# First loads and steps of a three-layer mixer in another order, the softmax over positions split off, state rows last in the first quarter

## The chip, the cores and the metric

The kernel runs on one core of one Trainium2 chip. The metric is the device time of that core in microseconds (us). In this text PE is TensorE, DVE VectorE, ACT ScalarE, POOL GpSimd and SP the engine that issues the loads and stores.

## The reference, cut to what matters

```python
def reference(x, state, moe_w_in, moe_w_out, moe_alpha, moe2_w_in, moe2_w_out):
    # x [4, 8, 512, 64], state [4, 8, 32, 64]
    s = 0.125 * x @ state.T                       # [4, 8, 512, 32]
    xread = softmax_over_states(s) @ state        # [4, 8, 512, 64]
    sread = softmax_over_positions(s.T) @ x       # [4, 8, 32, 64]
    t = concat([xread, sread], axis=2)            # 544 rows of a batch
    t = t.transpose(0, 2, 1, 3).reshape(4 * 544, 512)
    h = t @ moe_w_in                              # 512 -> 2048
    t = (max(h, 0) + moe_alpha * min(h, 0)) @ moe_w_out    # -> 512
    h = t @ moe2_w_in
    return (max(h, 0) + log1p(exp(-abs(h)))) @ moe2_w_out
```

A softmax has 1e-9 added to its sum. The four weights are 64-bit floats in memory; x, the state and alpha are 32-bit floats.

## The kernel before, in words

**Three layers in one pass.** Attention between 512 positions and 32 state rows of each of 8 heads and 4 batches gives 4 x 544 token rows of 512 numbers. Two feed-forward layers follow (m = 0 with leaky relu, m = 1 with softplus), each 512 to 2048 to 512. Each of their inner dimensions is worked through in NQ = 4 quarters of 512; in a quarter `hidden` computes a tile of 128 inner columns (fc = 0 to 3) for one block of 512 tokens (b = 0 to 3, the positions of a batch), or, for the block B, all 512 inner columns for the 128 state rows; `act` applies the nonlinearity and `out_part` multiplies by the second weight and adds into the running output. `out_part` runs LAG = 3 tiles behind.

**Accuracy.** TensorE's products are made of three: `mm3` (L136 to L138) multiplies high by high, low by high and high by low, and `split` makes the two parts, the high one on ACT (L142) and the low one on DVE or POOL (L145).

**Weights.** They come in 64 tiles of 128 x 512, each a load of 512 KB of 8-byte words into one of three staging buffers (`wload`, L188). `wconv` turns one into 32-bit floats: two steps on ACT (L202 exp, L203 top), three on DVE (L204, L205, L206) and one on POOL (L207), through one buffer `exp` and one buffer `top`. It then issues the next `wload`, which waits for the staging buffer. `wprep` (letter p) converts if needed and splits; the four tiles of the first weight in layer 0 (wi0h, wi0l, wi1h, wi1l for the first quarter) stay whole. The output weights of the first quarter (wo0 to wo3) follow them.

**Attention.** A step i is a batch and a group of four heads: i = 2 * batch + group, eight steps. It uses one of three sets of scratch tiles, i % 3; for i % 3 = 0 these are acc tiles, for 1 the tiles wo4 to wo6, for 2 further acc tiles and wi4, at7l. The parts, with their letters in the tables, are:

- x: `at_load_t` (L250), two loads of 256 KB of the transposed x; y: `at_load_x` (L254), two loads of x.
- s: `at_scores` (L269 to L275): eight matmuls give scores in PSUM, ACT copies them (L270), DVE takes their maximum over the positions (L271) and makes the bias (L272), ACT takes the exponent with its sum (L273), DVE adds the 1e-9 and takes the reciprocal (L274, L275).
- r: `at_rows` (L283 to L292): four transposes of the copied scores, the softmax over the states on DVE, ACT (L288) and POOL (L292).
- b: `at_back` (L299): transposes back and splits into at0h, at0l and so on. d: `at_read` (L308 to L330): transposes the exponents, multiplies by x (L314), scales (L323), transposes (L324), copies into the state rows (L330, srh).
- w: `sw_batch` (L238), the state times the first weight (tiles sw0h, sw0l and so on): `hidden` multiplies the probabilities by that product, so a block needs its own and its batch's steps.

**What sets the order.** Tables in the code do: LOADS and BEFORE list parts ahead of the first hidden tile, AMONG those ahead of the n-th hidden tile of the first quarter; SPLIT and SPLIT_FIRST say after which tiles a weight is prepared, SW_AHEAD and SW_LAST where the state-weight batches of later quarters go. A scheduler arranges each engine's queue from them once, when the program is built; each engine then runs its queue in order and waits on semaphores. All loads and stores stand in SP's queue.

## Time and profile of the kernel before

| quantity | us |
|---|---|
| median of three timed runs | 753.73 (753.58 to 754.25) |
| profiled execution, its own time | 752.3 |
| span of the profiled execution | 750.5 |
| PE busy (share of the span) | 727.6 (97%) |
| DVE busy | 425.3 (57%) |
| ACT busy | 423.2 (56%) |
| POOL busy | 170.5 (23%) |

The profiled execution is one run recorded by the hardware. Its span goes from the first to the last recorded instruction; 1.8 us of its time lie outside. The shares are averages over the whole span, so the rows further down take it stretch by stretch, and then instruction by instruction where an engine stands idle.

### The profile page before, as it was taken

The numbers are of one execution on the slowest core, as the hardware profiler recorded it, in microseconds if no ns is written. First come the engines' busy times: TensorE is split into PE (matmuls) and PEld (weight loads), VectorE is DVE, ScalarE is ACT, GpSimd is POOL, SyncE is SP. The second block draws the span as 40 slices with busy tenths as digits, with TensorE's granted clock in tenths as the row PEclk, the third lists the DMA queues.
The fourth block names the chain that finished last, engine by engine and source line by source line (L and its number), as shares of the span: only waits on it lengthen the run. The fifth ranks groups of instructions, "written<-read, shape, count | busy, mean of one in ns | idle before, by whom it ended". The sixth has DMA issues, their size and how long they took to land.

```text
span 750.5 us, 9504 instructions
## 1 busy us (share of the span) xinstructions
PE 727.6 (97%) x3580; PEld 561.7 (75%) x3580; DVE 425.3 (57%) x693; ACT 423.2 (56%) x764; POOL 170.5 (23%) x142
## 2 busy tenths in 40 slices
PE   5699998999999999999999999999999999999998
PEld 2267665777777777878888888888888888888886
DVE  4898657757778447885575224654257342333433
ACT  4778767735554335554677647755466354444560
POOL 2352332402142003452571003410044000000000
PEclk9989999999999999999999999999999999999999
DMA  9654313203211001220122001220010000001102
GB/s 323 221 174 156 107 44 115 85 7 108 83 57 57 0 1 58 86 82 1 56 79 91 0 1 57 84 85 1 0 57 0 1 1 0 1 1 56 57 15 112
DMA packets 16654, 47.27 MB, mean 63 GB/s; under 512 B 2016, under 2 KB 2016, under 8 KB 16608
## 3 DMA queue, kind: packets, MB, share of 16 engines
q1 hardware_dynamic: 16608, 46.66, 18.4%
q8 instruction: 28, 0.46, 0.3%
q14 instruction: 18, 0.15, 0.1%
HBM read 42.20 MB, written 4.46 MB: 62 GB/s over the span
## 4 chain that ended last, share of the span: by engine, by line
PE 94%; DVE 2%; ACT 2%; DMA 1%; issue 1%; POOL 0%; SPq 0%; ACTq 0%
PE pb L136 17%; PE pb L138 17%; PE pb L137 17%; PE pa L136 13%; PE pa L137 12%; PE pa L138 12%; PE pa L238 2%; PE pa L359 2%; PE pa L269 1%; DMA acc<-xt 1%; DVE top L204 1%; PE pa L367 0%; ACT exp L202 0%; PE pb L269 0%; ACT top L203 0%
## 5 line engine op out<-in xcount | busy, mean ns | idle before, releaser
L386 DVE SCALAR_TENSOR_TENSOR pa<-pa,tmp 128x512 f32<-128x512 f32 x68 | 47.4, 697 | 128.8 <-ACT tmp L385 128.8
L383 ACT ACTIVATE tmp<-pa 128x512 f32<-128x512 f32 x68 | 40.5, 596 | 92.7 <-PE pa L138 73.0
L429 DVE TENSOR_TENSOR acc<-pb,acc 128x512 f32<-128x512 f32 x102 | 67.4, 686 | 37.4 <-PE pb L138 37.4
L204 DVE SCALAR_TENSOR_TENSOR top<-stg,top 128x512 uint16<-128x512 uint16 x64 | 53.0, 828 | 46.8 <-ACT top L203 46.2
L207 POOL TENSOR_TENSOR cnv<-top,cnv 128x512 f32<-128x512 bf16 x48 | 56.4, 1175 | 101.0 <-DVE cnv L206 97.2
L379 DVE SCALAR_TENSOR_TENSOR pa<-tmp,rest,pa 128x512 f32<-128x512 f32 (+1 forms) x80 | 53.2, 671 | 25.7 <-ACT tmp L375 25.2
L202 ACT ACTIVATE exp<-stg 128x512 bf16<-128x512 bf16 x64 | 42.9, 671 | 38.7 <-DVE cnv L206 28.6
L375 ACT ACTIVATE tmp<-pa 128x512 f32<-128x512 f32 x68 | 40.2, 596 | 43.0 <-PE pa L138 36.4
L203 ACT ACTIVATE top<-exp,top_bias 128x512 uint16<-128x512 uint16 x64 | 46.1, 721 | 9.2 <-POOL cnv L207 5.5
L385 ACT ACTIVATE tmp<-tmp 128x512 f32<-128x512 f32 x68 | 42.9, 630 | 1.7
L384 ACT ACTIVATE tmp<-tmp 128x512 f32<-128x512 f32 x68 | 42.9, 631 | 1.5
L206 DVE SCALAR_TENSOR_TENSOR cnv<-stg,exp 128x512 f32<-128x512 uint32 x48 | 35.8, 745 | 13.0 <-POOL wo5l L145 4.1
L205 DVE TENSOR_SCALAR exp<-top 128x512 uint16<-128x512 uint16 x64 | 32.1, 502 | 1.1
L142 ACT ACTIVATE g1h<-pa 128x512 fp32r<-128x512 f32 x33 | 19.7, 596 | 20.8 <-DVE pa L386 12.4
L142 ACT ACTIVATE g3h<-pa 128x512 fp32r<-128x512 f32 x33 | 19.7, 596 | 19.3 <-DVE pa L379 9.6
L142 ACT ACTIVATE g0h<-pa 128x512 fp32r<-128x512 f32 x33 | 19.6, 594 | 19.1 <-DVE pa L379 10.2
L145 DVE TENSOR_TENSOR g3l<-pa,g3h 128x512 fp32r<-128x512 f32 x33 | 22.7, 689 | 13.4 <-ACT g3h L142 13.2
L145 DVE TENSOR_TENSOR g1l<-pa,g1h 128x512 fp32r<-128x512 f32 x33 | 22.7, 688 | 12.7 <-ACT g1h L142 12.3
L145 DVE TENSOR_TENSOR g0l<-pa,g0h 128x512 fp32r<-128x512 f32 x33 | 22.7, 688 | 10.5 <-ACT g0h L142 10.1
L145 DVE TENSOR_TENSOR g2l<-pa,g2h 128x512 fp32r<-128x512 f32 x33 | 22.7, 687 | 10.0 <-ACT g2h L142 9.9
L142 ACT ACTIVATE g2h<-pa 128x512 fp32r<-128x512 f32 x33 | 19.7, 597 | 14.5 <-DVE pa L386 7.6
L145 POOL TENSOR_TENSOR wo3l<-cnv,wo3h 128x512 fp32r<-128x512 f32 x5 | 6.5, 1294 | 76.1 <-ACT wo3h L142 75.9
(863 smaller groups left out, 2119.7 us busy)
## 6 DMA issues: line engine op xcount, KB each, us to landing
stg<-w1i SPq DMA_DIRECT2D x16, 511.8 KB, 4.0
stg<-w1o SPq DMA_DIRECT2D x16, 511.8 KB, 3.4
stg<-w2i SPq DMA_DIRECT2D x16, 511.8 KB, 3.9
stg<-w2o SPq DMA_DIRECT2D x16, 511.8 KB, 3.3
out<-acc SPq DMA_DIRECT2D x16, 256.0 KB, 2.0
acc<-xt SPq DMA_DIRECT2D x10, 256.0 KB, 4.8
acc<-xs SPq DMA_DIRECT2D x8, 256.0 KB, 5.3
wo4h<-xt SPq DMA_DIRECT2D x3, 256.0 KB, 3.5
```

Of the source, the lines that this page charges most:

```text
L136: nc.tensor.matmul(ps, lh, rh, start=start, stop=False)
L137: nc.tensor.matmul(ps, lh, rl, start=False, stop=False)
L138: nc.tensor.matmul(ps, ll, rh, start=False, stop=stop)
L142: nc.scalar.activation(h, src, AF.Copy)
L145: eng_l.tensor_tensor(out=l, in0=src, in1=h, op=ALU.subtract)
L202: nc.scalar.activation(e, top.bitcast(BF16), AF.Abs)
L203: nc.scalar.activation(tu, eu, AF.Relu, bias=top_bias, scale=TOP_SCALE)
L204: nc.vector.scalar_tensor_tensor(out=tu, in0=top, scalar=TOP_SIGN, in1=tu, op0=ALU.bitwise_and, op1=ALU.bitwise_or)
L207: nc.gpsimd.tensor_tensor(out=a, in0=t, in1=a, op=ALU.add)
L379: nc.vector.scalar_tensor_tensor(out=ps[:, cs], in0=t[:, cs], scalar=a, in1=ps[:, cs], op0=ALU.mult, op1=ALU.add)
L386: nc.vector.scalar_tensor_tensor(out=ps, in0=ps, scalar=0.0, in1=t, op0=ALU.max, op1=ALU.add)
L429: nc.vector.tensor_tensor(out=a, in0=ps, in1=a, op=ALU.add)
```

## The change

LOADS now brings the transposed x of steps 0 and 1 around the first weight tiles and x of step 0, and no more. BEFORE has 12 entries where it had 27: weights, scores, rows and transposes back of steps 0 and 1, the first state-weight batch and the load of step 2. The rest is spread over 13 entries of AMONG. A new part, letter e, `at_positions`, holds the softmax over the positions, which was the end of `at_scores`; it reads the copy of the scores, not PSUM. Its two small operations that make the bias and add the 1e-9, and the one of `at_rows` that adds the 1e-9, go from DVE to POOL. The block of the state rows is the last one in the first quarter instead of the fourth. In the first quarter conversions stop at 16 tiles. The state-weight batches of blocks 2 and 3 come after the hidden tiles 5 and 9, and the second quarter has a table of its own for preparing weights.

```diff
--- before.py
+++ after.py
@@ -43,11 +43,16 @@
 
 
 
-LOADS = "L0 x0 L0 y0 x1 L0 x2 y2 y1"
-BEFORE = "p0 s0 c0 s1 r0 p0 c0 r1 d0 b0 p0 x3 d1 y3 p0 w0 b1 p0 y4 s2 p0 r2 c0 x4 s3 w1 c0"
-AMONG = ("d2 r3 b2", "d3 s4 x5", "b3", "r4", "s5 y5 p0 d4 x6", "p0 r5 s6", "y6 d5 r6 b4 b5", "", "y7 x7 s7 d6", "b6 r7", "d7 b7")
-
-SPLIT_FIRST = (9, 10, 11, 12, 13, 14, 15, 16)
+LOADS = "L0 x0 L0 x1 L0 y0"
+BEFORE = "p0 s0 p0 s1 r0 p0 r1 x2 b0 p0 w0 b1"
+AMONG = (
+    "y1 e0 d0 s2 r2 p0", "x3 s3 e1 d1 p0 b2", "y3 y2 r3 p0", "b3 w1 p0",
+    "e2 d2 x4 y4", "e3 d3 x5 y5 s4 r4", "s5 r5 b4", "b5 e4 d4 x6 y6",
+    "e5 d5 x7 y7 s6 r6", "s7 r7 b6", "b7", "e6 d6", "e7 d7",
+)
+
+SPLIT_FIRST = (9, 10, 11, 12, 13, 14, 15)
+SPLIT_SECOND = (2, 3, 4, 5, 7, 9, 10, 12, 16)
 SPLIT = (1, 2, 4, 5, 7, 9, 10, 16)
 
 SW_AHEAD = (10, 13, 15)
@@ -261,17 +266,21 @@
     def at_scores(i):
 
         b, g = i // 2, i % 2
-        t, n2 = scratch(i), st_n[i % 3]
+        t = scratch(i)
         ps = bank(pool_s(i))
         for k in range(2):
             for hh in range(2):
                 r, o = slice(hh * D, (hh + 1) * D), col(g, k, hh)
                 nc.tensor.matmul(ps[o : o + NS], stf.f[r, head(2 * g + k, b)], t[k][r], start=True, stop=True)
         nc.scalar.activation(t[4], ps, AF.Copy)
-        nc.vector.tensor_reduce(out=n2[:, 0:1], in_=ps, op=ALU.max, axis=AX.X)
-        nc.vector.tensor_scalar(n2[:, 0:1], n2[:, 0:1], -SCALE, None, op0=ALU.mult)
-        nc.scalar.activation(t[5], ps, AF.Exp, bias=n2[:, 0:1], scale=SCALE, accum_out=n2[:, 1:2])
-        nc.vector.tensor_scalar(n2[:, 1:2], n2[:, 1:2], EPS, None, op0=ALU.add)
+
+    def at_positions(i):
+
+        t, n2 = scratch(i), st_n[i % 3]
+        nc.vector.tensor_reduce(out=n2[:, 0:1], in_=t[4], op=ALU.max, axis=AX.X)
+        nc.gpsimd.tensor_scalar(n2[:, 0:1], n2[:, 0:1], -SCALE, None, op0=ALU.mult)
+        nc.scalar.activation(t[5], t[4], AF.Exp, bias=n2[:, 0:1], scale=SCALE, accum_out=n2[:, 1:2])
+        nc.gpsimd.tensor_scalar(n2[:, 1:2], n2[:, 1:2], EPS, None, op0=ALU.add)
         nc.vector.reciprocal(n2[:, 1:2], n2[:, 1:2])
 
     def at_rows(i):
@@ -287,7 +296,7 @@
         nc.vector.tensor_tensor(out=e3, in0=p3, in1=m1.to_broadcast([P, 16, NS]), op=ALU.subtract)
         nc.scalar.activation(e1, e1, AF.Exp, scale=SCALE)
         nc.vector.tensor_reduce(out=s1, in_=e3, op=ALU.add, axis=AX.X)
-        nc.vector.tensor_scalar(s1, s1, EPS, None, op0=ALU.add)
+        nc.gpsimd.tensor_scalar(s1, s1, EPS, None, op0=ALU.add)
         nc.vector.reciprocal(s1, s1)
         nc.gpsimd.tensor_tensor(out=e3, in0=e3, in1=s1.to_broadcast([P, 16, NS]), op=ALU.mult)
 
@@ -454,6 +463,8 @@
             i = int(x[1:])
             if x[0] == "s":
                 at_scores(i)
+            elif x[0] == "e":
+                at_positions(i)
             elif x[0] == "r":
                 at_rows(i)
             elif x[0] == "d":
@@ -488,7 +499,7 @@
     for m in range(2):
         for q in range(NQ):
             first = m == 0 and q == 0
-            blocks = (0, 1, 2, B, 3) if first else (0, 1, B, 2, 3)
+            blocks = (0, 1, 2, 3, B) if first else (0, 1, B, 2, 3)
             n = 0
             for b in blocks:
                 for fc in range(4 if b < B else 1):
@@ -502,15 +513,16 @@
                     if len(todo) >= LAG:
                         out_part(*todo.pop(0))
                     todo.append((m, q, b, fc, g))
-                    wconv()
+                    if not first or nconv[0] < 4 * NQ:
+                        wconv()
                     if m == 0:
                         if n in SW_AHEAD and q < NQ - 1:
                             sw_batch(q + 1, SW_AHEAD.index(n))
-                        if first and b in (0, 1) and fc == 2:
-                            sw_batch(q, b + 2)
+                        if first and n in (5, 9):
+                            sw_batch(q, 2 + (n == 9))
                         if not first and n == SW_LAST:
                             sw_batch(q, B - 1)
-                    if n in (SPLIT_FIRST if first else SPLIT):
+                    if n in (SPLIT_FIRST if first else SPLIT_SECOND if (m, q) == (0, 1) else SPLIT):
                         wprep()
                     n += 1
     for job in todo:
```

The tables alone do not say where an instruction stands, since the scheduler arranges it. Three places of the built program follow, first before and then after. Operand names carry buffer numbers (pa and pb are PSUM banks); lines of after are 5 to 9 higher than the same lines of before (L136 is L141, L238 is L243, L283 is L292, L308 is L317).

PE around the first hidden tile (the matmuls with at0h, sw0h to at1h, sw1l; acc_99, acc_100 and at7l are steps 2 and 3's tiles, wi0h to wi1l the first weights, ex0h the state), before:

```order
L324 MATMUL pb_247<-ident,wo4h 128x128
L238 MATMUL pa_281<-wi1l,ex0h 32x512 x2
L269 MATMUL pb_363<-acc_95,ex0h 32x512 x2
L269 MATMUL pb_363<-acc_96,ex0h 32x512 x2
L283 MATMUL pa_342<-ident,wi4l 128x128 x4
L238 MATMUL pa_374<-wi0h,ex0h 32x512 x2
L238 MATMUL pa_374<-wi0l,ex0h 32x512 x2
L238 MATMUL pa_375<-wi1h,ex0h 32x512 x2
L238 MATMUL pa_375<-wi1l,ex0h 32x512 x2
L308 MATMUL pa_399<-ident,at7l 128x128 x4
L283 MATMUL pa_428<-ident,acc_99 128x128 x4
L136 MATMUL pa_449<-at0h,sw0h 128x512
```

and after:

```order
L243 MATMUL pa_204<-wi1l,ex0h 32x512 x2
L141 MATMUL pa_296<-at0h,sw0h 128x512
L142 MATMUL pa_296<-at0l,sw0h 128x512
L143 MATMUL pa_296<-at0h,sw0l 128x512
L333 MATMUL pa_243<-ident,acc_95 128x128
L141 MATMUL pa_296<-at1h,sw1h 128x512
L142 MATMUL pa_296<-at1l,sw1h 128x512
L143 MATMUL pa_296<-at1h,sw1l 128x512
L317 MATMUL pa_329<-ident,wo6l 128x128 x4
L274 MATMUL pb_318<-acc_95,ex0h 32x512 x2
L274 MATMUL pb_318<-acc_96,ex0h 32x512 x2
L323 MATMUL pb_335<-wo5h,wo6h 32x64 x8
```

Before, the scores of step 3 (acc_95, acc_96), the batch of block 1 (the two pairs L238) and the transposes of step 2's exponents (at7l) stand ahead of the first hidden tile; after, the first hidden tile comes right behind wi1l, and step 3's scores (L274) right behind it.

SP's queue, where step 3's loads are acc_95 and acc_96 from xt, and stg_64 to stg_66 are the staging buffers, before:

```order
L254 DMA acc_97<-xs 128x512
L254 DMA acc_98<-xs 128x512
L250 DMA acc_96<-xt 128x512
L188 DMA stg_66<-w1o 128x2047
L250 DMA acc_95<-xt 128x512
L254 DMA wo5h<-xs 128x512
L254 DMA wo5l<-xs 128x512
L188 DMA stg_64<-w1o 128x2047
L250 DMA wo4l<-xt 128x512
L188 DMA stg_65<-w1o 128x2047
```

and after:

```order
L193 DMA stg_65<-w1o 128x2047
L255 DMA acc_96<-xt 128x512
L193 DMA stg_66<-w1o 128x2047
L193 DMA stg_64<-w1o 128x2047
L255 DMA wo4l<-xt 128x512
L259 DMA acc_97<-xs 128x512
L259 DMA acc_98<-xs 128x512
L193 DMA stg_65<-w1o 128x2047
L255 DMA acc_95<-xt 128x512
L259 DMA wo5h<-xs 128x512
L259 DMA wo5l<-xs 128x512
```

Before, acc_95's load comes ahead of the loads into wo5h, wo5l and stg_64; after, it stands behind the second load into stg_65 of this list.

ACT's queue where the second gate tile's high half (g1h) is made, before:

```order
L202 ACTIVATE exp_75<-stg_65 128x512
L270 ACTIVATE wo6h<-pa_499 128x512
L142 ACTIVATE g0h<-pa_449 128x512
L203 ACTIVATE top_74<-exp_75,top_bias 128x512
L142 ACTIVATE wo2h<-cnv_69 128x512
L375 ACTIVATE tmp_72<-pa_512 128x512
L142 ACTIVATE at2h<-pb_440 128x512
L330 ACTIVATE srh<-pb_405 64x32 x4
L273 ACTIVATE wo6l,stn_84<-pa_499,stn_84 128x512
L323 ACTIVATE acc_95<-pb_476,stn_83 128x128
L375 ACTIVATE tmp_73<-pa_542 128x512
L142 ACTIVATE g1h<-pa_512 128x512
```

and after:

```order
L339 ACTIVATE srh<-pb_335 64x32 x4
L147 ACTIVATE at2h<-pa_362 128x512
L147 ACTIVATE wo1h<-cnv_68 128x512
L208 ACTIVATE top_74<-exp_75,top_bias 128x512
L282 ACTIVATE acc_100,stn_83<-acc_99,stn_83 128x512
L297 ACTIVATE acc_96<-acc_96 128x512
L384 ACTIVATE tmp_72<-pa_371 128x512
L384 ACTIVATE tmp_73<-pa_411 128x512
L207 ACTIVATE exp_75<-stg_65 128x512
L147 ACTIVATE wo2h<-cnv_69 128x512
L208 ACTIVATE top_74<-exp_75,top_bias 128x512
L147 ACTIVATE g1h<-pa_371 128x512
```

After, the second and third hidden tiles (tmp_72, tmp_73) are passed on next to each other, and a conversion's exp, a split and top stand between them and g1h; before, read-out parts and scores stood there.

## Rows read from the trace of the kernel before

**Rows 1.** Stretches: length, busy us of PE, PEld, DVE, ACT, POOL; clock, DMA.

```profile
0.00:38.15 38.15, 22.62 (x173) 9.49 (x174) 25.44 (x59) 24.21 (x51) 11.45 (x16) 0.95 0.77 269
38.15:92.90 54.75, 54.66 (x426) 36.60 (x424) 45.86 (x90) 42.13 (x96) 20.72 (x18) 0.97 0.44 145
92.90:121.50 28.60, 25.05 (x159) 16.92 (x158) 17.94 (x34) 19.78 (x44) 8.71 (x8) 1.00 0.22 74
121.50:345.00 223.50, 223.50 (x1064) 169.93 (x1065) 154.66 (x246) 117.17 (x202) 63.97 (x50) 1.00 0.18 57
```

**Rows 2.** Waits of PE, 0 to 130 us: total, times, longest.

```profile
PE pa L136 <- DVE g1l L145: 2.4, 1, 2.4
...
PE pa L136 <- ACT srh L330: 1.2, 1, 1.2
```

**Rows 3.** Timeline of PE: start, us, line, operands, count, idle before.

```profile
25.96 0.62 PE L238 MATMUL pa<-wi1l,ex0h 64*32 64x512 f32 x2 [1.38 <-POOL wi1l L207]
...
26.43 1.44 PE L269 MATMUL pb<-acc,ex0h 64*32 64x512 f32 x6
...
27.80 0.66 PE L283 MATMUL pa<-ident,wi4l 128*128 128x128 f32 x4
...
28.38 0.62 PE L238 MATMUL pa<-wi0h,ex0h 64*32 64x512 f32 x2
...
29.57 0.60 PE L238 MATMUL pa<-wi1l,ex0h 64*32 64x512 f32 x2
...
37.72 0.63 PE L138 MATMUL pa<-at1h,sw1l 128*128 128x512 f32 x1
...
104.45 0.62 PE L238 MATMUL pa<-wi2h,ex0h 64*32 64x512 f32 x2
...
105.47 0.50 PE L136 MATMUL pa<-at4h,sw4h 128*128 128x512 f32 x1
```

**Rows 4.** Stretch of 2 us around the first hidden tile; clock after POOL's busy time.

```profile
36.00:38.00 2.00, 2.00 (x6) 1.55 (x5) 2.00 (x8) 2.00 (x5) 0.31 (x2) 0.50 0.68 240
```

**Rows 5.** Page, groups: busy us, mean ns; conversion (L202 to L207), splits.

```profile
L204 DVE SCALAR_TENSOR_TENSOR top<-stg,top 128x512 uint16<-128x512 uint16 x64 | 53.0, 828 | 46.8 <-ACT top L203 46.2
...
L207 POOL TENSOR_TENSOR cnv<-top,cnv 128x512 f32<-128x512 bf16 x48 | 56.4, 1175 | 101.0 <-DVE cnv L206 97.2
...
L202 ACT ACTIVATE exp<-stg 128x512 bf16<-128x512 bf16 x64 | 42.9, 671 | 38.7 <-DVE cnv L206 28.6
...
L203 ACT ACTIVATE top<-exp,top_bias 128x512 uint16<-128x512 uint16 x64 | 46.1, 721 | 9.2 <-POOL cnv L207 5.5
...
L206 DVE SCALAR_TENSOR_TENSOR cnv<-stg,exp 128x512 f32<-128x512 uint32 x48 | 35.8, 745 | 13.0 <-POOL wo5l L145 4.1
...
L205 DVE TENSOR_SCALAR exp<-top 128x512 uint16<-128x512 uint16 x64 | 32.1, 502 | 1.1
...
L142 ACT ACTIVATE g1h<-pa 128x512 fp32r<-128x512 f32 x33 | 19.7, 596 | 20.8 <-DVE pa L386 12.4
...
L145 DVE TENSOR_TENSOR g1l<-pa,g1h 128x512 fp32r<-128x512 f32 x33 | 22.7, 688 | 12.7 <-ACT g1h L142 12.3
```

**Rows 6.** Timeline of DVE: third step of two successive conversions.

```profile
34.10 0.67 DVE L206 SCALAR_TENSOR_TENSOR cnv<-stg,exp 128x512 f32<-128x512 uint32 x1
...
41.10 0.68 DVE L206 SCALAR_TENSOR_TENSOR cnv<-stg,exp 128x512 f32<-128x512 uint32 x1
```

**Rows 7.** Timeline of the load queue (SP): first half of step 3.

```profile
20.29 0.38 SPq L250 DMA_DIRECT2D acc<-xt  x1
```

**Rows 8.** Page, DMA issues: KB each, us from issue to landing.

```profile
acc<-xt SPq DMA_DIRECT2D x10, 256.0 KB, 4.8
...
wo4h<-xt SPq DMA_DIRECT2D x3, 256.0 KB, 3.5
```

**Rows 9.** Groups by form, DVE and POOL: busy us, mean ns.

```profile
L272 DVE TENSOR_SCALAR stn<-stn 128x1 f32<-128x1 f32 x8 | 1.2, 148 | 0.1
...
L547 POOL MEMSET const-float32-1.0<- 128x1 f32 x1 | 0.1, 98 | 0.0
```

## The prediction

> **What bounds the kernel now.** I read the busy time of the engines by stretches first [rows 1]. From 121.5 to 345 us TensorE (PE) is busy for all 223.5 of 223.5 us. Nothing that this change does to an order can shorten that: from about 150 us to the end PE's queue is the same, instruction for instruction. What can be won or lost lies ahead of that. From 0 to 38.15 us, where the first hidden tile is finished, PE is busy for 22.62 us, so 15.5 are idle; from 38.15 to 92.9 it idles 0.09; and from 92.9 to 121.5 it idles 28.60 - 25.05 = 3.55. The waits of PE by releaser [rows 2] name these last 3.55 us: 1.2 for the copies of the state read-out on ACT (srh), 2.4 for the low half of a gate tile on DVE (g1l). Both stand around the state rows' block. So the question is how early PE can begin a row of matmuls without a hole. In that sense the start bounds the kernel, and behind it stand ACT and DVE, which prepare everything that PE reads: in 38.15 to 92.9 they are busy 42.13 and 45.86 of 54.75 us, 77% and 84% [rows 1]. They have room, but not much.
>
> **The change, part by part.** The sum is made against the profiled execution, 752.3 us, of which 1.8 lie outside the span of 750.5; the median of the three timed runs is 1.43 above it (753.73).
>
> *An earlier first hidden tile.* Its last operand in the new order is the low half of the second state-weight tile, and that hangs on the fourth weight tile, wi1l. In the kernel before PE gets that tile at 25.96 [rows 3]; less work stands ahead of it now (the read-out of step 1 and the scores of steps 2 and 3 are partly behind it), and walking the queues I find it at about 25.55, an estimate. Then come, in the order of ACT's and DVE's queues, the next weight tile's conversion up to its third DVE step and only then the split: 0.72 + 0.83 + 0.50 + 0.75 + 0.69 [rows 5], and one matmul of 0.43, from 37.72 to the end of the hidden tile at 38.15 [rows 3]. Sum 3.9, so 29.5 instead of 38.15. With four transposes that follow (some 0.5) PE stands at 30.0. But work that was done before 38.15 is now still open: the scores of step 3 (27.80 - 26.43, about 1.4), the transposes of its rows and those of step 2's exponents (0.58 each, 28.38 - 27.80), the read-out of step 1 (about 0.8, estimated from instruction counts), and the state-weight batch of block 1, between 1.0 (105.47 - 104.45, when all four weights are ready and four matmuls stand abreast) and 1.8 (28.38 to 30.17, two abreast) [rows 3]. I take 1.0, together 4.4. **Lead: 38.15 - 30.0 - 4.4 = 3.75 us.** Its bounds: 2.5 with the dearer batch and wi1l as late as before, 4.8 if wi1l comes 1 us earlier still.
>
> *The state rows' block at the end of the first quarter.* Its read-out now has block 3's matmuls as cover, and the 1.2 and 2.4 us of [rows 2] go: **3.55 us gained**. What covers them: the out-matmuls of block 3, twelve of the 512-column kind for each gate tile; if they run out, up to 2.4 come back.
>
> *A new wait for step 3's inputs.* This is what the move costs on the queue of loads. In the kernel before the first half of step 3's load is issued at 20.29 [rows 7]. Now it stands behind the load of a weight tile that has to wait for a staging buffer, which DVE's third step of the first output-weight tile sets free. That step I put at 28.7 (wi1l's successor, by the conversion's own steps), so the load goes out at about 29.15, since one issue takes 0.4. It lands 3.5 us later as the lone 256 KB load does, or 4.8 as such loads do in the middle [rows 8]: 32.7 to 34.0. PE's scores of step 3 stand directly behind the first hidden tile, and ahead of the second and third, so PE is held from 30.0 to **32.7: 2.7 us lost**, at most 4.0. I take the lower end because only the weight load of the moment is beside it. Behind the waiting scores stand the whole of block 0's remaining hidden tiles, which need nothing of step 3.
>
> *Waits for gate tiles and read-outs that stand behind conversions.* The weight conversion goes round through single buffers: 0.72 and 0.83 + 0.50 + 0.75 + 1.18 make 3.97 us [rows 5], with the handovers and one or two splits of 0.60 between them 5.1 to 5.6, an estimate; in the kernel before two successive third steps lie 41.10 - 34.10 = 7.0 apart [rows 6]. PE is now some 4 us ahead but the conversions aren't, and gate tiles stand behind them in ACT's queue: the second gate tile behind exp, a split and top (0.67 + 0.60 + 0.72 [rows 5]), then its own 0.60 [rows 5], 2.6 and with handovers 2.7 to 3.2 after DVE's third step. Third steps at 40.1, 50.8 and 60.0 give 43.25 for the second gate tile, 53.5 for the fourth and 63.25 for a read-out's copies. PE would be ready at 41.5, 52.1 and 61.7: **1.7, 1.4 and 1.55 us lost**. Later, where the softmax and read-outs of batches 2 and 3 come closer together, I take **1.0** more, near the 1.2 that such a copy cost before [rows 2]; between 0 and 1.6. For all four together (5.65) the bounds are 0, if the conversions keep step, and about 7.
>
> *State-weight batches of the second quarter.* They fall on a moment at which their four weights come one after the other, so pairs instead of fours: 1.79 instead of 1.02 [rows 3], **0.7 lost**; between 0 and 0.8.
>
> *The split softmax, and small operations on GpSimd.* The exponent of the positions is a function of its own now, but on ACT it stands at rows 7, 12 and 20 for the first three steps (6, 13 and 32 before): it is hardly put off. I cost it at nothing; what hides it is that PE has transposes and scores of other steps beside it, and uncovered it is 0.7. Twenty-four small operations go from DVE to GpSimd: 0.148 us each on DVE [rows 9], 8 of them a little more. That frees some 4 us of DVE over 100 us, none of it on the path by itself. What one costs on GpSimd the trace doesn't show; the nearest row is a fill of the same shape, 0.10 us [rows 9], and the far end is a tile-wide operation there, 1.18 [rows 5]. I take the near one, for the shape: nothing on the path, at the far end 1 us once, on step 0.
>
> The Trainium skill, "GPSIMD Engine Reference", section "Engine selection", speaks against that move: elementwise work belongs on VectorE, and on GpSimd two-input operations take about twice as long. [...]
>
> *The clock.* From 36 to 38 us PE is busy all the time and its granted clock reads 0.50 [rows 4], the lower of its two levels, 1.2 of 2.4 GHz, after 15.5 us of idle time in the 38 before [rows 1]. So the first hidden tile ran at half speed. In the new order PE idles for wi1l and for step 3's load just as it did, so I take the same loss. If the clock stays up, up to 1.5 us are gained.
>
> The sum: 3.75 + 3.55 - 2.7 - 5.65 - 0.7 = -1.75, that is 1.75 us slower: 754.05 for the profiled execution, and **755.5** for the median.
>
> **The rivals.** *The conversions keep step (the other side, faster).* All of the 5.65 us hang on ACT's queue in block 0 and 1. If a conversion's round takes under some 4.6 us instead of 5.1 to 5.6, the second gate tile is ready before PE at 41.5 and the later ones too. For it: ACT and DVE are busy only 77% and 84% there, and the order puts fewer softmax steps between conversions. Against it: the 7.0 us between third steps in the kernel before. It gives 7.3 - 2.7 - 0.7 = 3.9 faster: 749.8, and 748.3 with the clock up. *Half of these waits.* 1.1 faster, 752.6 to 753.8: within what can be told. *The load of step 3 comes at the far end and the stall at the quarter's end stays.* 1.3 + 2.4 more: 759.2. For it, the 4.8 of [rows 8]; against it, the cover of block 3's matmuls. *The change doesn't do what it says:* the softmax isn't put off (the order says so) and the earlier start only moves idle time about, so nothing that counts is different: 753.7.
>
> **How the numbers follow.** A measurement of this kernel can tell about 0.2%, 1.5 us, from no change: the bounds are 752.2 and 755.2. Chances: the forecast (754.5 to 757.5) 0.37, the conversions keep step 0.29, half of the waits 0.14, no effect 0.08, load and end stall 0.12. Faster takes the second case and a little of the third, 0.30; same takes most of the third, the fourth and the lower edge of the forecast, 0.26; slower the rest, 0.44. Since both signs hold much, the likeliest case's own range is 754.5 to 757.5; the range for 8 in 10 reaches from the first rival's 749.0 to 759.5.
>
> **What would show it.** In the profile of the changed kernel: the first hidden tile finished near 29.5; a PE wait of about 2.7 for a load of xt at the scores behind it; PE waits for gate tiles' splits near 43 and 53; no waits for srh and g1l of 1.2 and 2.4 around the state rows' block; from about 150 us on, the same busy time. The prediction is wrong if the conversions' third steps lie under 4.6 us apart, if step 3's load is issued before 27, or if the last waits of the quarter remain.

## The result and the profile of the changed kernel

The changed kernel takes 759.39 us (median of four runs, 758.49 to 761.15) against 753.65 for the kernel before: 5.7 us slower, a ratio of 1.0078 with a 95% interval of 1.0056 to 1.010. The prediction was 755.5, and the time lies at the upper end of its range of 749.0 to 759.5. The sign was right and the size was not: 1.75 slower were forecast.

The profiled execution is the longest of the four, 761.15 us with a span of 759.4, so its traces show 8.9 us more span than the kernel before, not 5.7. One thing that may differ among the executions is told under the hardware, at the end.

Both kernels by stretch, first the kernel before (length, busy us and instructions of PE, PEld, DVE, ACT, POOL, then clock, DMA share, GB/s; compare [rows 1]):

```profile
0.00:40.00 40.00, 24.47 (x208) 10.98 (x208) 27.17 (x61) 25.90 (x54) 13.30 (x17) 0.93 0.73 257
40.00:100.00 60.00, 58.73 (x454) 39.74 (x446) 50.09 (x99) 45.59 (x105) 20.21 (x18) 0.99 0.43 141
100.00:160.00 60.00, 57.63 (x288) 41.24 (x287) 37.16 (x62) 38.45 (x73) 18.64 (x15) 1.00 0.22 71
```

and the changed kernel:

```profile
0.00:40.00 40.00, 22.77 (x152) 9.56 (x153) 24.41 (x46) 21.30 (x42) 16.07 (x26) 0.92 0.65 228
40.00:100.00 60.00, 52.39 (x395) 36.06 (x394) 45.16 (x80) 45.58 (x102) 22.95 (x28) 1.00 0.49 160
100.00:160.00 60.00, 58.86 (x352) 38.56 (x351) 32.52 (x57) 35.65 (x73) 14.51 (x14) 1.00 0.13 45
```

PE idles 1.7 us more up to 40, 6.3 more from 40 to 100, and 1.2 less from 100 to 160, together 6.8 more. Up to 40 us ACT and DVE have done 4.6 and 2.8 us less than before; they are less busy, not more. The waits of PE in the changed kernel (us in total, times, longest) answer to [rows 2]:

```profile
PE pb L274 <- DMA acc<-xt: 11.7, 2, 7.1
PE pb L141 <- ACT g1h L147: 2.8, 2, 2.3
PE pb L141 <- ACT g3h L147: 1.6, 1, 1.6
...
PE pa L141 <- ACT srh L339: 0.9, 1, 0.9
```

The 7.1 us are the first load of all, which the kernel before has too; the other 4.6 are step 3's load. On PE's timeline (start, us, line, operands, count, idle before and its releaser) the places forecast are these:

```profile
30.27 0.50 PE L143 MATMUL pa<-at1h,sw1l 128*128 128x512 f32 x1 [1.19 <-DVE sw1l L150]
...
35.80 1.93 PE L274 MATMUL pb<-acc,ex0h 64*32 64x512 f32 x8 [4.60 <-DMA acc<-xt]
...
48.53 1.20 PE L141 MATMUL pb<-g1h,wo1h 128*128 128x512 f32 x4 [2.33 <-ACT g1h L147]
...
59.55 1.20 PE L141 MATMUL pb<-g3h,wo3h 128*128 128x512 f32 x4 [1.65 <-ACT g3h L147]
```

The first hidden tile is finished at 30.6 (before: 38.15); four transposes follow, and PE then stands until 35.8.

This wait and the next are tied to each other through ACT. L211 is a conversion's third step on DVE, L275 the copy of step 3's scores and L207 the exp with which the next conversion begins:

```profile
34.83 0.64 DVE L211 SCALAR_TENSOR_TENSOR cnv<-stg,exp 128x512 f32<-128x512 uint32 x1
37.80 0.60 ACT L275 ACTIVATE acc<-pb 128x512 f32<-128x512 f32 x1 [4.08 <-PE pb L274]
39.08 0.66 ACT L207 ACTIVATE exp<-stg 128x512 bf16<-128x512 bf16 x1
44.78 0.69 DVE L211 SCALAR_TENSOR_TENSOR cnv<-stg,exp 128x512 f32<-128x512 uint32 x1
```

ACT stands 4.1 us for the scores that wait for the load, the next exp comes behind their copy in ACT's queue, and two successive third steps lie 9.95 us apart. The second gate tile follows behind the later one.

There is a second loss, and it isn't idle time: the state-weight matmuls themselves take longer. PE's busy time on that one line, from 100 to 130 and 130 to 160 us, in the kernel before (length, PE busy and count, weight loads, clock, DMA share, GB/s):

```profile
100.00:130.00 30.00, 3.22 (x34) 0.50 (x34) 1.00 0.26 81
130.00:160.00 30.00, 2.17 (x30) 0.36 (x30) 1.00 0.19 61
```

and in the changed kernel:

```profile
100.00:130.00 30.00, 5.34 (x48) 0.80 (x48) 1.00 0.01 1
130.00:160.00 30.00, 4.25 (x32) 0.62 (x32) 1.00 0.26 88
```

5.39 us for 64 matmuls became 9.59 for 80, since one batch falls later. From 0 to 350 us the line has 23.30 before and 26.36 after: 3.1 us of PE time for the same 256 matmuls. With the 6.8 us of idle time that is 9.9, beside the 8.9 of the spans.

### The profile page after: what moved, and what is told of

Read it like the earlier page. It is cut to its first block, busy times and chain, and to the rows that moved or that the text cites. A ratio compares the mean times of both kernels' runs of the same rounds, so it can differ in the third digit from the quotient of the medians.

```text
span 759.4 us, 9485 instructions
## 1 busy us (share of the span) xinstructions
PE 729.7 (96%) x3580; PEld 561.7 (74%) x3580; DVE 424.1 (56%) x669; ACT 424.2 (56%) x764; POOL 178.2 (23%) x166
## 4 chain that ended last, share of the span: by engine, by line
PE 88%; DVE 4%; ACT 3%; DMA 3%; POOL 1%; issue 1%; SPq 0%
PE pb L141 16%; PE pb L142 16%; PE pb L143 16%; PE pa L141 12%; PE pa L143 12%; PE pa L142 12%; PE pa L243 2%; DMA acc<-xt 2%; PE pa L368 2%; DVE top L209 1%; ACT top L208 1%; POOL cnv L212 1%; DMA stg<-w1i 1%; PE pa L376 0%; DVE exp L210 0%
## 5 line engine op out<-in xcount | busy, mean ns | idle before, releaser
L207 ACT ACTIVATE exp<-stg 128x512 bf16<-128x512 bf16 x64 | 42.8, 669 | 42.5 <-DVE cnv L211 30.0
L384 ACT ACTIVATE tmp<-pa 128x512 f32<-128x512 f32 x68 | 40.1, 594 | 39.0 <-PE pa L143 33.9
L211 DVE SCALAR_TENSOR_TENSOR cnv<-stg,exp 128x512 f32<-128x512 uint32 x48 | 35.7, 744 | 12.9 <-POOL wo5l L150 4.0
```

## The experiments

Each part was undone in the changed kernel, or done alone in the kernel before. "Before" is the kernel before in the same series of runs, 752.96 to 753.26. The changed kernel was timed only in the series of the result (before: 753.65), and its four executions spread over 2.7 us, so differences from it of 1 to 2 us are uncertain. The order of the queues is made anew by the scheduler for every version, so a run tells what an edit does through that order too.

### Undone in the changed kernel

**Step 3's load earlier (a_x3).** The load now goes into a tile that step 0's read-out still writes, so some of step 3's scores are other numbers.

```diff
-BEFORE = "p0 s0 p0 s1 r0 p0 r1 x2 b0 p0 w0 b1"
+BEFORE = "p0 s0 p0 s1 r0 p0 r1 x2 b0 x3 p0 w0 b1"
...
```

(and x3 is gone from AMONG.)

> The changed kernel with the load of step 3's transposed x two places earlier in the tables; in SP's queue its first half then goes out ahead of the load of the fourth output-weight tile's staging buffer, at about 10 us. Theory A (the changed kernel loses by that load): the 4.6 us wait for it goes, and with it most of the stretch at half clock behind it (some 2 us); part comes back in the wait for the second gate tile. About 754.5, between 752.5 and 756. Rival B (the conversions in ACT's and DVE's queues set the pace, the load only sits in front of the same stall): the wait for the second gate tile grows by what the load gave back; 757.5 to 759.5.

758.47, 0.9 less than the changed kernel, with executions (757.24 to 759.18) that overlap with those of it. The 4.6 us wait for the load is gone, and PE stands at the next instructions of its queue for a copy on ACT:

```profile
34.38 0.65 PE L323 MATMUL pb<-wo5h,wo6h 128*32 128x64 f32 x16 [3.05 <-ACT wo6h L318]
```

Behind the load stood another wait of two thirds its size. PE's clock also falls a second time (stretches of 2 us; clock third from the end):

```profile
36.00:38.00 2.00, 2.00 (x9) 1.71 (x8) 1.89 (x4) 1.17 (x3) 1.84 (x3) 0.50 0.47 156
58.00:60.00 2.00, 2.00 (x6) 1.62 (x5) 0.00 (x0) 1.35 (x3) 1.17 (x1) 0.50 0.48 154
```

In half-microsecond stretches that read about 0.50 PE is busy for 9.1 us here and 4.7 in the changed kernel; half of the difference, 2.2 us, is an estimate of what that takes back. The time lies in the rival's range, but not for its reason: the wait for the second gate tile did not grow, it fell to 0.5.

**Step 0's read-out and step 3's load both earlier (a_d0x3).** The load meets step 0's row probabilities, which are still read, so those are other numbers.

```diff
-BEFORE = "p0 s0 p0 s1 r0 p0 r1 x2 b0 p0 w0 b1"
+BEFORE = "p0 s0 e0 p0 s1 r0 p0 d0 r1 x2 x3 b0 p0 w0 b1"
...
```

(and e0, d0 and x3 are gone from AMONG.)

> The changed kernel with step 0's softmax over positions and read-out put back ahead of step 1's, so that the tile that step 3's load goes into is free early, and with that load right behind; the scores of step 3 then stand ahead of the first hidden tile's matmuls again. Theory A (the load's late issue is the loss): its wait goes and, since the load isn't early at the cost of anything else, the changed kernel gets 3 to 4 us faster, 755 to 756.5. Theory D (ACT's and DVE's queues, the weight conversions in them above all, set the pace of block 0, whatever PE waits for first): the wait moves to a gate tile or a read-out copy, 757.5 to 759.

757.92, 1.5 less. The wait for the load is gone again and others took its place: 2.0 for a scaled read-out, 1.8 for the second gate tile, 1.6 for a state-weight split; PE is busy at the lower clock for 9.2 us here too. Taking the late load away gave 0.9 and 1.5 us by the medians, not its 4.6. How much of the rest went into the lower clock and how much into the waits behind the load, the two runs don't separate.

**Most of the conversion of four weights left out (a_noconv).**

```diff
+        if 4 <= i < 8:
+            nc.vector.tensor_scalar(a, low, REST, None, op0=ALU.mult)
+            ...
+            return
```

> The changed kernel with most of the conversion of the first quarter's four output weights left out: one DVE step of 0.7 us writes the tile, the two ACT steps, two DVE steps and the GpSimd step are not done, so these four weights have other values. Theory D (conversions set the pace in block 0): the waits for gate tiles of 2.3 and 1.6 us go and with them 4 us or more, 753 to 755.5. Theory A (the load of step 3): that wait stays or shrinks a little, since the scheduler puts the load's users later: 757.5 to 758.5.

761.08, 1.7 more than the changed kernel, although ACT, DVE and GpSimd had less to do. The wait for step 3's load is gone, the one for the second gate tile fell to 0.5, the one for the fourth grew to 3.0, and new ones of 2.5 (at1l) and 1.8 came. The 4 us that theory D put on the conversions did not come. But with the work gone the scheduler also built another order, with PE busy at the lower clock for 7.0 us instead of 4.7, so the run neither prices the conversions nor clears them. In the changed kernel itself the chain of work that leads to the wait for the fourth gate tile, at 59.5, runs from 43 us on through the conversions' steps on DVE, GpSimd and ACT. That part of theory D stays open.

**The state rows' block back in fourth place (a_st4).** The limit on conversions and the second quarter's table for the splits stay as in the changed kernel.

```diff
-            blocks = (0, 1, 2, 3, B) if first else (0, 1, B, 2, 3)
+            blocks = (0, 1, 2, B, 3) if first else (0, 1, B, 2, 3)
```

> The changed kernel with the state rows' block in the fourth place of the first quarter again. If the block's place at the end was worth the 3.55 us of waits that the kernel before had around it: the waits for the state read-out's copies (1.2) and for the low half of a gate tile (2.4) come back, 763. If it was worth nothing in the new order, because the read-outs are late or early anyway: 759.4, within 1.

757.51: 1.9 faster by the medians (756.62 to 758.70 against 758.49 to 761.15), where the forecast had the move as a gain. PE idles more, 60.00 - 55.97 = 4.0 us against 1.1 from 100 to 160, and the state-weight line takes less, 5.45 us against 9.59:

```profile
100.00:160.00 60.00, 55.97 (x358) 39.50 (x357) 39.94 (x64) 41.54 (x82) 20.15 (x17) 1.00 0.22 71
```

```profile
100.00:130.00 30.00, 3.27 (x48) 0.54 (x48) 1.00 0.11 36
130.00:160.00 30.00, 2.18 (x32) 0.36 (x32) 1.00 0.32 105
```

The first line is all of PE's work, the other two that line alone. The move buys 2.9 us of waits and pays 4.1 in matmuls: 1.25 lost from 100 to 160 by the profile, 1.9 by the timed runs. Before 40 us the two differ as well, with nothing of the move in it: PE waits 2.5 us for step 3's load here and 4.6 in the changed kernel's profile, so part of the 1.9 may be that load.

**The small operations back on DVE (a_dve).**

```diff
-        nc.gpsimd.tensor_scalar(n2[:, 0:1], n2[:, 0:1], -SCALE, None, op0=ALU.mult)
+        nc.vector.tensor_scalar(n2[:, 0:1], n2[:, 0:1], -SCALE, None, op0=ALU.mult)
```

(and so the other two).

> The changed kernel with the 24 small operations on DVE again as before the change. On GpSimd they take 0.31 to 0.40 us in the profile of the changed kernel, on DVE 0.15 to 0.24. The scheduler, with other durations, also puts the load of step 3 one place earlier, ahead of one weight load. Theory C (the small operations on GpSimd cost time on the path, by their own length and because GpSimd's last conversion step stands behind them): 2 to 3.5 us faster than the changed kernel, 756 to 757.5, and wi1l is ready 0.6 earlier. Theory A alone: 1 us faster by the load's place, 758.4. Rival: none of it is on the path, 759.4.

762.70: 3.3 slower. GpSimd is the better place for them, against all three expectations.

### Done alone in the kernel before

**The state rows' block last (b_stlast).** The limit on conversions and the second quarter's table for the splits belong to it, since the first quarter's weights must stay until the state rows have used them.

```diff
-            blocks = (0, 1, 2, B, 3) if first else (0, 1, B, 2, 3)
+            blocks = (0, 1, 2, 3, B) if first else (0, 1, B, 2, 3)
```

> The kernel before with only the state rows' block put last in the first quarter, and what that asks for: no conversion beyond 16 tiles in that quarter, one weight split less there and the second quarter's own table for the splits. If the block's place is worth the waits of 1.2 and 2.4 us: 750.1. If the splits that are put off to the second quarter make PE wait there, the gain comes back: 753 to 754.

753.53 against 753.26, a ratio of 1.0005 (0.9997 to 1.0014): nothing. From 100 to 160 PE no longer waits for g1l at all, so the wait of 2.4 is gone. The wait of 1.2 for srh is not; PE first in the kernel before, then here:

```profile
94.13 0.50 PE L136 MATMUL pa<-at4h,sw4h 128*128 128x512 f32 x1 [1.18 <-ACT srh L330]
93.31 0.50 PE L137 MATMUL pa<-at4h,sw4h 128*128 128x512 f32 x1 [1.18 <-ACT srh L331]
```

It stands ahead of block 2's first hidden tile, which comes before the state rows' block in either place, so the move could not take it away. The state-weight line takes 8.50 us from 100 to 160 instead of 5.39. What the place gives in waits, PE gives back in matmuls that run in pairs or pieces instead of four abreast.

**The three tables (b_tables).**

```diff
-LOADS = "L0 x0 L0 y0 x1 L0 x2 y2 y1"
+LOADS = "L0 x0 L0 x1 L0 y0"
...
+    "y1 d0 s2 r2 p0", "x3 s3 d1 p0 b2", "y3 y2 r3 p0", "b3 w1 p0",
+    "d2 x4 y4", "d3 x5 y5 s4 r4", "s5 r5 b4", "b5 d4 x6 y6",
```

> The kernel before with the three tables of the change alone (loads, steps ahead of the first hidden tile, steps among the tiles), the softmax over positions in one piece, its small operations on DVE and the state rows' block in fourth place. If the tables bring the loss that is left when the state rows' block is put back (757.5 against 753.3): 756.5 to 758.5, with the waits for step 3's load and the second and fourth gate tile. If the split softmax and GpSimd bring it: within 1 of 753.3.

762.80 against 753.05: 9.75 slower, twice what was looked for. So something else in the change must gain.

**The softmax as a part of its own and its small operations on GpSimd (b_pool).**

```diff
-        nc.vector.tensor_reduce(out=n2[:, 0:1], in_=ps, op=ALU.max, axis=AX.X)
+        nc.vector.tensor_reduce(out=n2[:, 0:1], in_=t[4], op=ALU.max, axis=AX.X)
-        nc.vector.tensor_scalar(n2[:, 0:1], n2[:, 0:1], -SCALE, None, op0=ALU.mult)
+        nc.gpsimd.tensor_scalar(n2[:, 0:1], n2[:, 0:1], -SCALE, None, op0=ALU.mult)
...
```

(The exponent reads the copy t[4] too, and the two operations that add the 1e-9 go to GpSimd.)

> The kernel before with the softmax over positions as a part of its own right behind the scores, reading the copy of the scores, and its two small operations and the one of the rows' softmax on GpSimd. Theory C (these operations, 0.31 to 0.40 us there, and the maximum that now waits for the copy of 0.6, lie on the path to the first hidden tile): 1 to 2 us slower than before, 754.3 to 755.5. Rival: they are covered, 753.3 within 0.5.

747.95: 5.1 faster, a ratio of 0.9928 (0.9915 to 0.994). Theory C falls. Two runs took it apart.

**The copy alone (b_pos),** with the small operations left on DVE:

> The kernel before with the softmax over positions reading ACT's copy of the scores instead of PSUM, still right behind the scores and with its small operations on DVE. Theory S (the gain of the run with both is that DVE's in-order queue no longer stands at small operations that wait for ACT's exponent, and with it the splits behind them): nothing gained by the copy alone, 752.5 to 754, and the waits of 1.4 and 0.7 us for stn stay. Rival P (the PSUM bank comes free earlier, or the maximum is cheaper from SBUF): 748 to 751.

751.16, 1.8 faster than 752.98 (0.9968 to 0.9985 as a ratio), between the ranges of theory S and of rival P. The waits for stn stay, as S had it, with 1.4 and 0.6.

**GpSimd alone (b_gponly),** with the maximum and the exponent still reading PSUM:

> The kernel before with only the 24 small operations on GpSimd; the maximum and the exponent still read PSUM. Theory S (DVE's queue freed of waiting): most of the 5.1 us that the run with both gained, 747.5 to 750, and the waits for stn gone. Rival P (the copy does it): 752.5 to 754.

745.78: 7.2 faster (0.989 to 0.9917). The 24 operations of 0.15 to 0.24 us are the larger gain, and both together (5.1) are less than this one alone. Of the kernel before I had left three waits aside (us in total, times, longest):

```profile
PE pa L308 <- ACT at7l L273: 1.9, 1, 1.9
PE pa L136 <- DVE stn L272: 1.4, 1, 1.4
...
PE pa L283 <- DVE stn L274: 0.7, 1, 0.7
```

They stand between 30 and 35.4 us, ahead of the first hidden tile. With GpSimd none of them is left, the first hidden tile begins at 30.15 instead of 35.42, with all the work that was ahead of it still ahead:

```profile
29.30 0.66 PE L308 MATMUL pa<-ident,at7l 128*128 128x128 f32 x4
29.79 0.60 PE L283 MATMUL pa<-ident,acc 128*128 128x128 f32 x4
30.15 0.48 PE L136 MATMUL pa<-at0h,sw0h 128*128 128x512 f32 x1
```

What changed on DVE is the order. Its queue in the kernel before, with the conversion of the first output weight (L204), step 2's maximum (L271), a small operation of the softmax and the split that block 1 needs (sw2l):

```profile
26.69 0.69 DVE L204 SCALAR_TENSOR_TENSOR top<-stg,top 128x512 uint16<-128x512 uint16 x1 [2.03 <-ACT top L203]
...
28.96 0.68 DVE L271 TENSOR_REDUCE stn<-pb 128x1 f32<-128x512 f32 x1
...
33.17 0.14 DVE L274 TENSOR_SCALAR stn<-stn 128x1 f32<-128x1 f32 x1
...
34.69 0.68 DVE L145 TENSOR_TENSOR sw2l<-pa,sw2h 128x512 fp32r<-128x512 f32 x1
```

and with GpSimd:

```profile
23.16 0.68 DVE L271 TENSOR_REDUCE stn<-pb 128x1 f32<-128x512 f32 x1
...
26.42 0.67 DVE L145 TENSOR_TENSOR sw2l<-pa,sw2h 128x512 fp32r<-128x512 f32 x1
...
27.74 0.69 DVE L204 SCALAR_TENSOR_TENSOR top<-stg,top 128x512 uint16<-128x512 uint16 x1
```

In the kernel before the maximum stands behind a conversion at which DVE stood for 2.03 us; with GpSimd maximum and split stand ahead of that conversion, 5.8 and 8.3 us earlier. My reason, that DVE stands at the small operations themselves, isn't in the trace: L274 at 33.17 has no idle time ahead of it. PE also keeps its clock (stretches of 2 us; clock third from the end):

```profile
30.00:32.00 2.00, 2.00 (x30) 1.46 (x32) 2.00 (x4) 1.34 (x4) 1.37 (x3) 1.00 0.16 55
...
36.00:38.00 2.00, 2.00 (x39) 1.47 (x38) 2.00 (x6) 2.00 (x6) 1.34 (x3) 1.00 0.74 203
```

where [rows 4] has 0.50. It falls later instead, to 0.50 from 116 to 118. PE is busy at the lower level for 6.1 us in the kernel before and for 3.5 here, so the clock gives some 1.3 of the 7.2, an estimate from half of the difference. What part of the 7.2 us is the 4 us of DVE's time and what part the other order that the scheduler makes, the runs don't separate.

**The early half of the tables (b_early)** has the two first tables, and the later steps where they stood:

> The kernel before with the first two tables of the change (loads and the steps ahead of the first hidden tile) and the steps that these leave out put ahead of the first three tiles; the later steps stand where they stood before. Theory E (an early first tile with little done ahead of it is what costs): most of the 9.6 us that all three tables cost, 757 to 762.8. Rival L (the later steps' places cost it): 752 to 754.5.

755.50 against 752.96: 2.5 slower, between the ranges of theory E and of rival L.

**The late half (b_late)** has the kernel's own start, and the steps of batches 1 to 3 where the change puts them:

```diff
-AMONG = ("d2 r3 b2", "d3 s4 x5", "b3", "r4", "s5 y5 p0 d4 x6", "p0 r5 s6", ...
+    "r3 b2", "", "", "b3", "d2 p0", "d3 x5 y5 s4 r4 p0", "s5 r5 b4", "b5 d4 x6 y6",
```

> The kernel before with its own loads and steps ahead of the first hidden tile, and the steps of batches 1 to 3 among the tiles where the change puts them. Theory L (the steps of later batches come too late or too close together there): 757 to 762.8. Theory E (it is the early start): 752 to 754.5.

759.51: 6.6 slower. The halves make 9.1 of the 9.75, and the late one is the dear one. The time is in theory L's range, but the early half costs something too. Ten us each from 50 us on, of the kernel before:

```profile
50.00:60.00 10.00, 10.00 (x52) 7.32 (x51) 9.28 (x17) 6.12 (x15) 3.51 (x3) 1.00 0.41 140
60.00:70.00 10.00, 9.91 (x82) 6.99 (x81) 8.49 (x21) 8.20 (x17) 3.40 (x3) 1.00 0.33 105
```

and of b_late:

```profile
50.00:60.00 10.00, 9.99 (x80) 7.23 (x80) 5.44 (x8) 7.03 (x13) 3.64 (x3) 1.00 0.45 149
60.00:70.00 10.00, 6.59 (x62) 3.96 (x61) 8.43 (x19) 7.01 (x21) 1.69 (x2) 0.93 0.65 210
```

While PE is busy from 50 to 60, at first with block 0's gate tiles, DVE, which prepares batch 1 in the kernel before (9.28 of 10 us), is busy 5.44. Then the steps come together, each with its chain of scores, copy, maximum, exponent and transposes, and PE is busy 6.59 of 10. Of the 3.4 us that it idles there, 2.2 are a wait for a load of x ahead of such scores, so the late loads have their part in it.

### Put together

**b_gp_early,** GpSimd with the early half of the tables:

> The run with the small operations on GpSimd alone (745.8), and with it the early start of the run before this one but one. If the early start costs through DVE's queue standing at those operations: little is lost here, 744 to 747. If it costs whatever DVE does: 750 to 756.

751.02, 5.2 slower than GpSimd alone. The early start costs with the small operations on GpSimd too, so DVE's queue standing at them is not the reason.

**b_pool_half2** was meant as a part of that:

> The run with the copy and GpSimd, and from the tables of the change one piece: the scores and rows of step 2, the load of step 4, the scores of step 3 and block 1's state-weight batch go from ahead of the first hidden tile into the list ahead of it among the tiles, behind the weights and ahead of nothing else. Theory T (an earlier first tile with less done ahead of it loses more in block 0 and 1 than it gains): 749.5 to 754. Rival (the tables' loss is only that they bring the read-out of step 0 and the load of step 3 late): 747 to 748.5.

747.42 against 747.95. But PE's, DVE's and ACT's queues came out as in b_pool, up to names of buffers: the scheduler put the steps back. The run tells nothing on the theory and is a second reading of b_pool.

**The state rows' block last, with the copy and GpSimd (b_pool_stlast):**

> The run with the copy and GpSimd, and the state rows' block last in the first quarter with what that asks for; in this order the second quarter's state-weight batches stay in one piece but for one. Theory B (the block's place saves its waits and costs only where the batches fall into halves): the 2.7 us of waits between 100 and 160 us go and nothing is paid: 745 to 746. Rival (the place is worth nothing by itself): 748 within 0.6.

744.81, a ratio of 0.9889 (0.9877 to 0.9902) to the kernel before and 3.1 less than b_pool. Here the state-weight line stays at 4.30 us from 100 to 160 in both, and the move gains; 2.0 of the 3.1 are PE's waits in that stretch. **With GpSimd alone (b_gp_stlast):**

> The run with the small operations on GpSimd alone (745.8), and the state rows' block last in the first quarter with what that asks for. If the 2.4 us wait for g1l at 121 us goes and the second quarter's state-weight batches stay whole: 743 to 744.5. If the batches fall into halves: 745.5 to 747.

746.18 against 745.78: nothing again, and that line goes from 4.30 to 7.41 us. In all four pairs the move gains 2.0 to 2.9 us of PE's waits from 100 to 160, and its worth goes with the line: +3.1 us there and no gain (the kernel before, and GpSimd alone), +4.1 and a loss (the changed kernel), 0 and a gain (b_pool).

b_pool_stlast is 8.2 us faster than the kernel before and 14.6 faster than the changed one.

## Why the prediction missed, step by step

- **What the parts are worth** in the runs: tables +9.75, copy and GpSimd -5.1, together 4.65; a_st4, which has both (and the limits and places of batches and splits that go with the move), is 4.3 above the kernel before. The state rows' move adds 1.9 in that order. The sum, 6.2 to 6.5, stands beside 5.7 measured.
- **The failed step: the state rows' block and the state-weight batches.** The sum had +3.55 for the first and -0.7, at most -0.8, for the second: 2.85 gained. In the profile 100 to 160 gives 1.2 of waits and the line costs 3.1 over all: 1.8 lost. That is 4.7 us of miss in one pair of terms, more than the 3.9 between forecast and median. The 3.55 was too large from the start: its 1.2 for srh is not at the state rows' block, as b_stlast shows, and the four pairs gained 2.0 to 2.9. I had counted one batch in pairs; in the built order three of the second quarter's batches fall into pairs or pieces, and I looked only at the first. Undoing the move made the kernel 1.9 faster by the medians, and surely not 3.6 slower.
- **The first hidden tile: right, late by 1.1.** 30.6 instead of 29.5. PE gets the fourth weight at 26.10 instead of 25.55, and from there to the end of the tile it takes 4.5 us instead of 3.9. On DVE a maximum of the split softmax (L280) stands directly ahead of that weight's third step, and one of the rows' softmax (L295), for which the sum had no term, stands between the next conversion's second step and its third:

```profile
23.52 0.68 DVE L280 TENSOR_REDUCE stn<-wi4l 128x1 f32<-128x512 f32 x1
24.11 0.68 DVE L211 SCALAR_TENSOR_TENSOR wi1l<-stg,exp 128x512 f32<-128x512 uint32 x1
...
28.33 0.68 DVE L295 TENSOR_REDUCE stm<-pa 128x16 f32<-128x512 f32 x1
28.93 0.68 DVE L211 SCALAR_TENSOR_TENSOR cnv<-stg,exp 128x512 f32<-128x512 uint32 x1
```

  The small operation on GpSimd ahead of the fourth weight's last step, 0.59 us long, ended 0.1 after DVE's part was done and cost no more than that.
- **Step 3's load: right place, too cheap, and not worth its size.** Issued at 30.07 (29.15 forecast), landed after 5.7 us where I took 3.5 and at most 4.8: 4.6 of wait instead of 2.7. I named the weight load ahead of it on SP as its cause, and that load does go out at 29.69, right ahead of it. There is a second bound that I did not see: the tile is step 0's until its read-out is done, and that ends at 28.6. But taking the wait away gained 0.9 and 1.5 only.
- **Gate tiles and read-outs: right places, 5.65 forecast, 6.3 more idle time from 40 to 100 measured.** 2.33 for 1.7, 1.65 for 1.4, both 5 to 6 us later than forecast. The third step that I put at 40.1 came at 44.78, since ACT stood for step 3's scores with that conversion's exp behind it; the sum has the load's wait and these waits as separate terms. In a_x3, without the load's wait, that third step came at 41.92 and the wait for the second gate tile fell to 0.5. That conversions set these waits fits the trace, but a_noconv did not bear it out, so this cause stays open. What b_late shows is that the spread of the later steps costs by itself.
- **The softmax and GpSimd at nothing: wrong.** They are worth 5.1 in the kernel before and the small operations 3.3 in the changed one. I reasoned that 4 us of DVE over 100 aren't on the path by themselves. That another order of DVE's queue comes with them, in which the maximum and the splits no longer stand behind a conversion that waits, I did not ask, though PE's waits for stn and for the exponent stood in the profile that I read. The other three terms of the sum, 3.75 - 2.7 - 5.65 = -4.6, met the 4.3 of a_st4, though the tables alone cost 9.75. The walk went through the changed order, so it may have held the gain without naming it; but the wait for the load measured 4.6 and gave 0.9 and 1.5 when it was taken away, so the agreement of these three is at least in part luck.
- **Their time on GpSimd: wrong end.** (Groups by form: busy us, mean ns, idle before.)

```profile
L299 POOL TENSOR_SCALAR sts<-sts 128x16 f32<-128x16 f32 x8 | 3.2, 401 | 9.5 <-DVE sts L298 9.1
L281 POOL TENSOR_SCALAR stn<-stn 128x1 f32<-128x1 f32 x8 | 2.5, 316 | 7.2 <-DVE stn L280 7.2
L283 POOL TENSOR_SCALAR stn<-stn 128x1 f32<-128x1 f32 x8 | 2.4, 305 | 5.7 <-ACT acc L282 2.7 <-ACT wo6l L282 2.5
```

  I took 0.10, from a fill; on DVE they take 0.15 to 0.24. The Trainium skill's "GPSIMD Engine Reference", "Engine selection", puts elementwise work on VectorE, and of GpSimd it says that one-input operations run at roughly line rate there. These have one input, and at this size they took about twice as long, so the trace doesn't bear out the second. Nor was the first right for the kernel's time: it became shorter with them on GpSimd, in both orders (b_gponly, a_dve).
- **The clock: right for the changed kernel.** It falls to 0.50 at 33 to 34 us, much as before, and is back at 1.00 by 42. In the experiments it was not the same, and part of what they gained or lost is the clock.
- **The rivals.** "The conversions keep step" was wrong in sign. The one with the load at its far end and a stall at the quarter's end gave 759.2; the load came so, the stall did not, and the batches cost as much, so its number met the measured 759.39 by luck. "Doesn't do what it says" failed to see that the reading and the engine of the softmax could count where its place did not.

## What to carry to other kernels

Small operations moved to another engine change the order of the queue that they leave; look for what stands there behind an instruction that waits (here the softmax's maximum and the splits, behind a conversion), and who waits for that, before such a move is priced at nothing. When a move saves waits, count the instructions that it rearranges over the whole stretch, since matmuls that no longer run abreast cost as much as a wait and show as busy time. An early start gained nothing here, where the work that it postpones then came in one piece: compare the preparing engines' busy time by stretch, and look for the one in which they idle. When a wait is taken away and the time hardly moves, compare the granted clock by stretch as well as the next wait.

## What the hardware showed that was not expected

**A load ends with most DMA engines idle.** The changed kernel's step 3 load was issued at 30.07. Stretches of 1 us (columns as above; the last three are clock, DMA share, GB/s):

```profile
32.00:33.00 1.00, 0.00 (x0) 0.00 (x0) 0.56 (x2) 0.98 (x2) 0.93 (x1) 1.00 1.01 371
33.00:34.00 1.00, 0.00 (x0) 0.00 (x0) 1.00 (x2) 0.72 (x2) 0.92 (x2) 0.84 0.07 27
34.00:35.00 1.00, 0.00 (x0) 0.00 (x0) 1.00 (x4) 0.00 (x0) 0.01 (x1) 0.50 0.07 27
```

From 33 us on the DMA share is 0.07, which is 1.1 of 16 engines on average, at 27 GB/s, until the load lands at 35.8. The bulk had ended nearly 3 us earlier. In a_st4's profile, where SP's queue is the same up to there, PE waited 2.5 us for this load and not 4.6. Executions of the changed kernel spread over 2.7 us, of which this may be a part; that was not tried.

**The same matmuls at two and three times the price.** A state-weight batch whose matmuls with all four weights start within 0.04 us of each other took 1.02 us in the kernel before [rows 3]. In the changed kernel one batch stands in three pieces on PE, at 122.2, 123.5 and 126.5, and the next in two, at 130.4 and 134.4, and each piece took about 1.05, whether it held two of the matmuls or twelve. Nothing in a count of instructions shows the difference.
